# Four numbers of a hand-made instruction plan: the place of the last weight stores, and how far ahead loads are issued

## The chip, the core and the metric

The kernel runs on one core of a Trainium2 chip. The core has TensorE (PE, matrix products; PEld is its loading of the stationary operand), VectorE (DVE), ScalarE (ACT), GpSimd (POOL) and SyncE (SP). Here SP does nothing but issue transfers between memory and the core's buffers; 16 DMA engines carry them out. Each engine works through its own list of instructions in order and waits at an instruction until what it needs is there. The metric is device time of one launch in microseconds (us); the kernel before takes 1144.37 us, the median of 3 runs (1144.27 to 1144.45).

## What is computed

Two layers, each an attention block and a feed-forward block, run twice with the same weights, on 2048 rows of 640 numbers (float32). Cut to what matters:

```python
def _A_ref(x, wqkv, wo):              # 32 heads of 20, window of 8 rows, 2 apart
    qkv = x @ wqkv
    idx = pos[:, None] - off[None, :]                # off = 0, 2, ..., 14
    logits = einsum("bhsd,bhswd->bhsw", q, k[idx]) * scale   # masked where idx < 0
    attn = softmax(logits)
    return einsum("bhsw,bhswd->bhsd", attn, v[idx]) @ wo

def _B_ref(x, w1, b1, w2, b2):        # 640 -> 1536 -> 640
    y = layernorm(x)
    h = gelu(y @ w1 + b1)
    return h @ w2 + b2

x = x + _A_ref(layernorm(x), wqkv, wo)
x = x + _B_ref(layernorm(x), w1, b1, w2, b2)
x = x + _A_ref(layernorm(x), wqkv, wo)
x = x + _B_ref(layernorm(x), w1, b1, w2, b2)
```

## The kernel before, in words

**Numbers as pairs.** Every matrix operand is held as a pair of float16 numbers, a high part and the rest ("hi" and "lo"), and a product is three passes over such pairs. Weights come as float32, are split on the chip (ACT makes hi, DVE makes lo, both at line 475 and 476), and the pairs of the feed-forward weights are written to a scratch array `mw` in memory: 12 blocks of w1 (`mw[0][f]`) and 12 of w2 (`mw[1][f]`), each 320 KB. This is `prep_m`; its store is the transfer at line 517. Every feed-forward block later loads them back, block by block, at line 864.

**Units and stages.** The 2048 rows are 4 units of 512 rows (4 tiles of 128); over two layers that makes 8 unit-stages n = 0 to 7. Each has a layer norm, a product with wqkv (`qkv`, line 648 on PE), spilling of q, k and v to memory and fetching with shifted rows (lines 671 and 690), attention on DVE for 4 groups of heads (lines 732 to 770), the product with wo (line 805), a second layer norm, and a feed-forward part (`mlp`). Normalised rows are turned by a transposing transfer (line 620, `yT<-w`; line 793, `yT<-ohl`).

**One feed-forward part.** `mlp` runs over 12 blocks e of the 1536 inner columns. Block j = 12 * part + e needs a `c1` load (w1) for its inner product (line 871, `ps<-yT,c`, 15 matmuls), then GELU and hi on ACT (877, 880), lo on DVE (882), and a `c2` load (w2) for its outer product (line 892, `acc<-c,act`), which adds into five accumulator banks over all 12 blocks. Unit 0 of layer 1 is done as two parts of two tiles each (parts 0 and 1, inner matmuls of 256 columns), the next five units as one part each; the last two units are done together by another scheme (`pair`, lines 1073 and 1108). After the units from the fourth on, ACT copies the accumulator banks back to the rows (lines 916 and 926, priority `DRAIN`) and, for the next one, the rows into the banks (lines 853 and 855, priority `FILL`).

**Buffers.** There are 3 buffers `c1` and 3 buffers `c2`. Splitting uses them too: block f of w1 is split into a `c1` buffer and block f of w2 into a `c2` buffer, which come free when the stores to `mw` have landed. The users of `c1` and of `c2` get buffers in a fixed order: the 12 blocks of the splitting first, then the loads 0, 1, 2, ... of the feed-forward parts.

**The order of everything** is made before the launch by the class `Plan`. Each step is added with its engine, an estimated duration, a priority (lower goes first), what it needs, gives and uses. `Plan.run` then plays a simple model of the engines and the transfers, always takes the step that can start first (at the same time the one of lower priority), and emits the instructions of each engine in that order. The estimated times go no further than the order: on the chip each instruction waits only for the results and buffers that it needs, and for those ahead of it on its engine. Four things in this class matter here:

- A transfer marked `lazy` (rows of x, weights, bias, the stores to `mw`, the `c1` and `c2` loads) may not start in the plan before the transfers planned so far are within `AHEAD` us of being done. The others (spills, fetches of q, k and v, transposes, outputs) may.
- `SPARE[engine]` is added to the planned landing of a transfer for a step of that engine that needs it.
- `prio` of the splitting store is `prio - 5`, with `prio = 10 + f`: 5 for the first block, 16 for the last. `c1` and `c2` loads have -250 + j (+ 1.5 for c2), fetches -300 + group, spills -310 + n, the transposes of the feed-forward's layer norm -150 + n.
- The priorities of ACT's copies between rows and accumulator banks are `FILL` and `DRAIN`. Other steps of ACT near them: GELU -430, hi of GELU -440, the exponential of attention -450 + group, the copies before and after the product with wo (lines 817 and 822) -600 + n and -700 + n.

```python
            if o["lazy"]:
                t = max(t, seen - self.AHEAD + sum(x[0] * x[1] for q in queues.values() for x in q)
                        + sum(v["move"][0] * v["move"][1] for _, v in soon))
```

Of the kernel before, what the change touches and what calls it, by code (L numbers as in the profile page):

```python
# [18 lines left out]
NF = F // P  # L19
# [20 lines left out]

AHEAD = 1.5

# [23 lines left out]
PAIRS = ("qk", "pv", "ad", "o", "sub", "at", "hlo", "yl", "xb", "ol", "wq", "lo", "lm")  # L66

TURN = 2.7
FILL, DRAIN = -420, -700

THROUGH = (("sa", 29),)
LOP = ((29, -460),)
# [2 lines left out]
class Plan:  # L75
# [8 lines left out]
    SWITCH = 1.3  # L84


    AHEAD = 3.0
    REACH = 0.75
    LAND = 0.9
    RAMP = 0.2  # L90

    SPARE = {"pe": 2.0, "act": 1.5, "dve": 1.5, "pool": 0.7, "sp": 0.0}

    SHARE = 1.08

# [26 lines left out]
    def run(self):  # L122
# [64 lines left out]
        def start(o):  # L187
            t = clock[o["eng"]]
# [3 lines that stand above are left out]
            if o["pair"] and o["eng"] == "dve":  # L192
                t = max(t, port)
            for k in o["need"]:
                e, w, moved = when[k]
                w = w + (self.LAG["sp"] + self.SPARE[o["eng"]] if moved else self.LAG[e] if e != o["eng"] else 0.06 * (e != "pe"))
                t = max(t, w)
# [80 lines left out]
def packet_time(n):  # L278
    return 0.0075 + n / 26.9e3
# [11 lines left out]
def sliding_dilated_then_mlp_kernel(  # L291
# [18 lines left out]
    nc = tc.nc  # L310
# [41 lines left out]
    def tile_of(pool, key):  # L352
        return T[pool][plan.slot[pool, key]]
# [52 lines left out]
    mw = [[dram.tile([P, 2, D], HT, name=f"mw{i}{f}") for f in range(NF)] for i in range(2)]  # L406
# [16 lines left out]
    def dma(kb, prio, emit, need=(), give=(), use=(), by="sp", packet=4 * D):  # L423
        lazy = give[0][0] in ("x", "sq", "st", "c1", "c2", "zero", "mw", "raw", "rows", "d1", "mt") or give[0] in ("b1", "b2")
        plan.add(by, 0.1 if by == "act" else 0.38, prio, emit, need, give, use, move=(kb * 1e3 / 16 / packet, packet_time(packet)), lazy=lazy)
# [4 lines left out]
    def mm(cols, n, prio, emit, need=(), give=(), use=()):  # L430
        plan.add("pe", cols / 2400.0 + 0.0028 * n, prio, emit, need, give, use)
# [63 lines left out]
    def prep_rows(name, prio, src, hi, lo, use=()):  # L495
        key = (through[name], name)

        def load():
            st = tile_of(*key)
            w = src()  # L500
            nc.sync.dma_start(st.rearrange("p (k c) -> p k c", k=w.shape[1]) if len(w.shape) == 3 else st, w)

        dma(P * D * 4 / 1e3, prio, load, need=[("ev", 0, M - 1, 0)], give=[("st", name)], use=[key],
            packet=4 * P if name[0] == "m" and not name[2] else 4 * D)
        a, v = split(hi, lo, lambda: tile_of(*key))
        act(D, prio, a, need=[("st", name)], give=[("hi", name)], use=[key, *use])
        dve(D, next(p for n, p in LOP if blocks.index(name) < n), v, need=[("hi", name)], give=[("lo", name)], use=[key, *use])
# [4 lines left out]
    def prep_m(f, i, prio):  # L512
        ck = (f"c{i + 1}", ("prep", f))
        src = (lambda: B_w2[f * P:(f + 1) * P]) if i else (
            lambda: B_w1.rearrange("(k p) c -> p k c", p=P)[:, :, f * P:(f + 1) * P])
        prep_rows(("m", f, i), prio, src, lambda: tile_of(*ck)[:, 0], lambda: tile_of(*ck)[:, 1], [ck])
        dma(328, prio - 5, lambda: nc.sync.dma_start(mw[i][f], tile_of(*ck)),
            need=[("lo", ("m", f, i))], give=[("mw", f, i)], use=[ck])

    def turn(prio, t, name, key, nk, yk):  # L520
# [309 lines left out]
    def mlp(at, b, t0, t1):  # L830
# [28 lines left out]
        for e in range(NF):  # L859
# [7 lines left out]
            def inner(ck=ck, pk=pk):  # L867
# [6 lines left out]

            mm(3 * KD * nt, 15, j - 1.0 - AHEAD, inner, need=[*ready, ck, *split_done] + [("hhi", j - 2)] * (e > 1), give=[("hp", j)],
               use=[yk, ck, pk])
# [155 lines left out]
    def pair():  # L1032
# [68 lines left out]
        def first(bank, wt, todo, start, prio, need, give, use):  # L1101

            def product():
                ps = tile_of(*bank)
                k = 0
                for w0, z in todo:
                    for a, c in PASS:
                        nc.tensor.matmul(ps, wt()[:, a, w0:w0 + P], z(c), start=start and k == 0, stop=k == 3 * len(todo) - 1,  # L1108
                                         skip_group_check=True)
                        k += 1  # L1110

            mm(3 * len(todo) * BANK, 3 * len(todo), prio, product, need=need, give=give, use=[bank, *use])
# [3 lines left out]
        def yb(k):  # L1116
            return lambda c: transposed(yk)[:, c * KD + k]

        for e in R:
# [3 lines left out]
            if e == 0:  # L1123
                rows_in("P1", -284, lambda e: mw[1][e][:, :, :HALF], lambda e: [("mw", e, 1)])
            wt = partial(tile_of, *ck)
            after = [("wop", n1, M - 1, 1)] if e < 3 else []
            first(pk, wt, [(k * P, yb(k)) for k in range(KH)], True, j - 1.0 - AHEAD, [*ready, ck, *after] + [("hi", ("P1", e - 2))] * (e > 1),
                  [("P1", e)], [yk, ck])
            act(BANK, -441, lambda pk=pk, e=e: nc.scalar.activation(A21[e], tile_of(*pk), AF.Copy), need=[("P1", e), *free["pr"]],
                give=[("s1", e)], use=[pk])  # L1130
            first(pk, wt, [(k * P, yb(k)) for k in range(KH, KD)], False, j - 1.1 - AHEAD, [("s1", e)], [("C11", e)], [yk, ck])
            gelu(A11[e], partial(tile_of, *pk), e, ("h11", e), [("C11", e), *free["wo"]], [pk])
# [21 lines left out]
        for e in R:  # L1154
# [16 lines left out]
            B52, B51 = 10 * P, 11 * P  # L1171
            pr = j - 1.0 - AHEAD
            act(BANK, -436, lambda e=e, bk=bk: nc.scalar.activation(tile_of(*bk), A21[e], AF.Copy), need=[("s1", e), ("P1", NP - 1)],
# [174 lines left out]
```

## Time and profile before

| | |
|---|---|
| time, median of 3 runs | 1144.37 us |
| the profiled execution | 1147.83 us, of which the span from first to last instruction is 1146.1 us |
| PE busy | 1137.1 us, 99% of the span |
| DVE busy | 1038.4 us, 91% |
| ACT busy | 606.6 us, 53% |
| POOL busy | 113.2 us, 10% |
| DMA engines busy, queue of SP | 69.9% of 16 engines' span, 234.36 MB |
| mean granted clock of PE | 0.998 |

How to read the profile's lines in what follows. A row of the timeline gives the start in us, the time it covers, engine, line of the code, operation, output and inputs by the program's names (buffer numbers left out, so `c` is a buffer `c1` or `c2`), how many instructions are merged, and in brackets the idle time before it with what ended that. SPq rows are SP issuing transfers: their time is that of the issue, not of the transfer. A row of the windows gives, for a stretch of time, the busy time of each engine with its number of instructions, then the granted clock of PE as a share of full speed, the mean busy share of the DMA engines, and GB/s. A row of the waits gives who waited for whom, the total us, how often, and the longest.

### The profile page before, as it was taken

Reading aid. Unit: us, or ns where it says so; the run is one execution under the profiler, and the core shown is the slowest. Engines: PE = TensorE matmul, PEld = TensorE weight load, DVE = VectorE, ACT = ScalarE, POOL = GpSimd, SP = SyncE. Lnnn points to the kernel's source line nnn. Section 1 sums busy time; section 2 is a strip of 40 time slices with the busy share of each in tenths; the row PEclk is TensorE's granted clock in tenths of the full one; section 3 lists DMA queues with packets and bytes.
Section 4 is the critical chain, followed back from the end, with each engine's and each line's share of the span. In section 5 each row is a group of like instructions: output and inputs, shape, how many; then the busy total and the mean of one; then the engine's idle time right before and its main releaser. Section 6 shows DMA issues by size and latency. Waiting matters only on the chain.

```text
span 1146.1 us, 17470 instructions
## 1 busy us (share of the span) xinstructions
PE 1137.1 (99%) x6812; PEld 628.4 (55%) x6812; DVE 1038.4 (91%) x1028; ACT 606.6 (53%) x1131; POOL 113.2 (10%) x94
## 2 busy tenths in 40 slices
PE   9999999999999999999999999999999999999998
PEld 6444446567565465546555555556455556555476
DVE  7999999999899999999999999999999993847972
ACT  6485336536365275734537662479347445657720
POOL 1010000211111102110112012012111000000000
PEclk9999999999999999999999999999999999999999
DMA  9999998978976477576655965569686555974201
GB/s 318 307 299 266 329 302 244 321 264 244 239 189 232 140 221 213 178 207 198 186 187 176 221 190 164 175 188 192 164 247 183 175 171 156 217 239 122 65 24 69
DMA packets 239791, 235.47 MB, mean 205 GB/s; under 512 B 139020, under 2 KB 195164, under 8 KB 239708
## 3 DMA queue, kind: packets, MB, share of 16 engines
q1 hardware_dynamic: 239708, 234.36, 69.9%
q8 instruction: 53, 0.87, 0.3%
q14 instruction: 30, 0.25, 0.1%
HBM read 157.55 MB, written 44.78 MB: 177 GB/s over the span
## 4 chain that ended last, share of the span: by engine, by line
PE 72%; DVE 3%; DMA 1%; issue 0%; ACT 0%; DVEq 0%
PE acc L892 18%; PE ps L871 17%; PE ps L648 17%; PE ps L805 10%; PE acc L1073 4%; PE ps L1108 3%; PE ps L1073 2%; DMA yT<-w 1%; DVE yT L1020 1%; DVE pr L1005 1%; PE acc L1108 1%; DVE wq L1194 0%; DVE wq L1182 0%; DVE v L1195 0%; DVE xf L1196 0%
## 5 line engine op out<-in xcount | busy, mean ns | idle before, releaser
L648 PE MATMUL ps<-wq,yT 128*128 128x480 f16 (+1 forms) x1950 | 391.0, 363 | 1.5 <-DMA yT<-w 1.1
L648 PEld LDWEIGHTS <-yT 128*128 128x128 f16 x1950 | 189.3, 98 | 200.8 <-DMA yT<-w 1.4
L892 PE MATMUL acc<-c,act 128*128 128x512 f16 (+1 forms) x1728 | 249.3, 299 | 2.3 <-DMA c<-mw 1.6
L871 PE MATMUL ps<-yT,c 128*128 128x512 f16 (+1 forms) x1260 | 247.8, 350 | 0.0
L892 PEld LDWEIGHTS <-act 128*128 128x128 f16 x1728 | 136.1, 98 | 108.8 <-issue 1.9
L871 PEld LDWEIGHTS <-c 128*128 128x128 f16 x1260 | 120.9, 98 | 107.3 <-DMA c<-mw 0.3
L732 DVE TENSOR_TENSOR pr<-qk 128x2560 f32<-128x2560 f32 x64 | 179.5, 2808 | 0.0
L758 DVE TENSOR_TENSOR pr<-sm,v 128x2560 f32<-128x2560 f32 x64 | 179.1, 2818 | 0.3
L736 DVE TENSOR_REDUCE sm<-pr 128x128 f32<-128x2560 f32 x64 | 179.2, 2801 | 0.0
L665 ACT ACTIVATE ev<-ps 128x480 f32<-128x480 f32 x128 | 72.6, 568 | 177.2 <-PE ps L648 157.5
L877 ACT ACTIVATE act<-ps,b 128x512 f32<-128x512 f32 (+1 forms) x84 | 52.4, 624 | 172.9 <-PE ps L871 170.2
L766 DVE TENSOR_TENSOR pr<-pr 128x640 f32<-128x640 f32 (+1 forms) x128 | 143.1, 1150 | 0.3
L805 PE MATMUL ps<-wo,yT 128*128 128x320 f16 x960 | 131.7, 299 | 0.0
L805 PEld LDWEIGHTS <-yT 128*128 128x128 f16 x960 | 93.8, 98 | 37.4
L780 POOL TENSOR_TENSOR ohl<-w,ohl 128x640 f16<-128x640 f32 x24 | 34.9, 1456 | 425.9 <-DVE pr L732 171.6
L882 DVE TENSOR_TENSOR act<-act 128x512 f16<-128x512 f32 (+1 forms) x84 | 51.0, 609 | 16.0 <-ACT act L880 15.9
L587 POOL TENSOR_TENSOR ln<-ln,half 128x2 f32<-128x2 f32 (+1 forms) x31 | 36.2, 1173 | 276.6 <-ACT ln L584 276.6
L625 POOL TENSOR_TENSOR xf<-xf,b 128x640 f32<-128x640 f32 x24 | 37.3, 1558 | 144.6 <-DVE pr L732 58.4
L880 ACT ACTIVATE act<-act 128x512 f16<-128x512 f32 (+1 forms) x84 | 47.5, 565 | 3.4 <-PE acc L892 1.5
L610 ACT ACTIVATE w<-xf,ln 128x640 f32<-128x640 f32 x53 | 47.5, 909 | 2.7 <-DVE w L618 2.1
L570 ACT ACTIVATE junk<-xf 128x640 f16<-128x640 f32 x57 | 41.8, 733 | 12.9 <-DVE xf L814 8.0
L618 DVE TENSOR_TENSOR w<-w,w 128x640 f16<-128x640 f32 x56 | 45.7, 830 | 2.1 <-ACT w L616 2.1
(200 smaller groups left out, 984.1 us busy)
## 6 DMA issues: line engine op xcount, KB each, us to landing
c<-mw SPq DMA_DIRECT2D x174, 320.0 KB, 3.6
spill<-ev SPq DMA_DIRECT2D x64, 480.0 KB, 3.6
qk<-spill SPq DMA_DIRECT2D x32, 880.0 KB, 6.0
v<-spill SPq DMA_DIRECT2D x32, 880.0 KB, 5.3
qk<-spill SPq DMA_DIRECT2D x32, 320.0 KB, 3.6
act<-in_B_w_dram SPq DMA_DIRECT2D x24, 320.0 KB, 4.9
mw<-c SPq DMA_DIRECT2D x24, 320.0 KB, 4.7
pr<-in_B_w_dram SPq DMA_DIRECT2D x24, 320.0 KB, 4.1
```

The source lines that it names most:

```text
L648: nc.tensor.matmul(ps, transposed(yk)[:, a * KD + k, t * P:(t + 1) * P], wq[:, b, k, g, i0:i1], start=first and j == 0, stop=last and j == ...
L665: act(3 * GC, -400 + n, lambda i=i, pk=pk, ek=ek: nc.scalar.activation(tile_of(*ek)[:, :, i], tile_of(*pk)[:, :3 * GC].rearrange("p (a c) ...
L732: nc.vector.tensor_mul(tile_of(*pk), w[:, HALO + m + t0:HALO + m + t0 + EH, None, :].to_broadcast([P, EH, W, GC]), windows(w, t0, [GC, W], ...
L736: dve(E, G - 0.7, lambda pk=pk, t0=t0: nc.vector.tensor_reduce(lg(t0, t0 + EH).rearrange("p t w h -> p (t w h)"), tile_of(*pk).rearrange(" ...
L758: nc.vector.tensor_mul(tile_of(*vk).rearrange("p t w (h d) -> p t (w h) d", d=DH), lg(t0, t0 + EH).rearrange("p t w h -> p t (w h)")[:, :, ...
L766: dve(EH * w * GC, G - 0.9, lambda vk=vk, w=w: nc.vector.tensor_add(tile_of(*vk)[:, :, 0:w], tile_of(*vk)[:, :, 0:w], tile_of(*vk)[:, :, w ...
L805: nc.tensor.matmul(tile_of(*pk)[:, :D // 2], transposed(yk)[:, a * KD + k, t * P:(t + 1) * P], wo[:, b, k, c * D // 2:(c + 1) * D // 2], s ...
L871: nc.tensor.matmul(tile_of(*pk)[:, :nt], tile_of(*ck)[:, a, k * P:(k + 1) * P], transposed(yk)[:, c * KD + k, t0 * P:t1 * P], start=i == 0 ...
L877: act(nt, -430, lambda pk=pk, h32=h32, e=e: nc.scalar.activation(tile_of(*h32)[:, :nt], tile_of(*pk)[:, :nt], AF.Gelu_apprx_tanh, bias=b1[ ...
L882: dve(nt, -1000, lambda h32=h32, hk=hk: nc.vector.tensor_sub(tile_of(*hk)[:, 1, :nt], tile_of(*h32)[:, :nt], tile_of(*hk)[:, 0, :nt]), nee ...
L892: nc.tensor.matmul(accs[k][:, c0:c0 + n], tile_of(*hk)[:, a, (i - t0) * P:(i - t0 + 1) * P], tile_of(*wk)[:, c, w0:w0 + n], start=first, s ...
L1073: nc.tensor.matmul(tile_of(*to(i))[:, :HALF], hl()[:, a, i * P:(i + 1) * P], row(c), start=start and (a, c) == PASS[0], stop=(a, c) == PAS ...
```

## The change

Three numbers of the plan, and the priority of one pair of stores. `AHEAD` goes from 3.0 to 2.0 us, `SPARE` of ACT from 1.5 to 1.0 us, `DRAIN` from -700 to -450. The stores of the last block of the splitting (f = 11, of `mw[0][11]` and `mw[1][11]`) get priority -260 instead of 16; the other 22 keep theirs. No step of the plan is added or removed, and no data moves that did not move before; only orders change.

```diff
-FILL, DRAIN = -420, -700
+FILL, DRAIN = -420, -450
...
-    AHEAD = 3.0
+    AHEAD = 2.0
...
-    SPARE = {"pe": 2.0, "act": 1.5, "dve": 1.5, "pool": 0.7, "sp": 0.0}
+    SPARE = {"pe": 2.0, "act": 1.0, "dve": 1.5, "pool": 0.7, "sp": 0.0}
...
-        dma(328, prio - 5, lambda: nc.sync.dma_start(mw[i][f], tile_of(*ck)),
+        dma(328, -260 if f > NF - 2 else prio - 5, lambda: nc.sync.dma_start(mw[i][f], tile_of(*ck)),
             need=[("lo", ("m", f, i))], give=[("mw", f, i)], use=[ck])
```

## The prediction, made before the changed kernel was built

> **What bounds the kernel now.** I read the page first, then PE's waits, then windows and timelines of PE, DVE and SP around each wait.
>
> ```profile
> span 1146.1 us, 17470 instructions
> PE 1137.1 (99%) x6812; PEld 628.4 (55%) x6812; DVE 1038.4 (91%) x1028; ACT 606.6 (53%) x1131; POOL 113.2 (10%) x94
> ```
>
> PE is busy in all but 9.0 us, and the change leaves PE's work as it is. So a gain can only be idle time of PE, or time in which it runs slowly. These are its waits, all of them:
>
> ```profile
> PE acc L892 <- DMA c<-mw: 1.6, 2, 1.3
> PE acc L1269 <- POOL ident L447: 1.3, 1, 1.3
> PE ps L648 <- DMA yT<-w: 1.1, 1, 1.1
> PE acc L892 <- DVE act L882: 0.7, 1, 0.7
> PE acc L531 <- DVE w L606: 0.3, 1, 0.3
> PE ps L648 <- DVE yT L539: 0.2, 1, 0.2
> ```
>
> L1269, L531 and L539 belong to the first microseconds, before any feed-forward part. The others stand in two places, both in the first feed-forward unit. The first place, on PE:
>
> ```profile
> 234.37 1.80 PE L871 MATMUL ps<-yT,c 128*128 128x256 f16 x15
> ...
> 237.99 0.72 PE L892 MATMUL acc<-c,act 128*128 128x512 f16 x4 [0.73 <-DVE act L882]
> 239.97 1.05 PE L892 MATMUL acc<-c,act 128*128 128x512 f16 x4 [1.26 <-DMA c<-mw]
> 240.81 3.16 PE L871 MATMUL ps<-yT,c 128*128 128x256 f16 x15
> ...
> 244.90 1.80 PE L871 MATMUL ps<-yT,c 128*128 128x256 f16 x15
> ...
> 248.16 1.04 PE L871 MATMUL ps<-yT,c 128*128 128x256 f16 x8
> ```
>
> Undisturbed, one block (15 inner and 12 outer matmuls) takes 248.16 - 244.90 = 3.26 us. The inner products that start at 234.37 and 244.90 are two blocks apart, so 6.52 us of work took 10.53: **4.0 us are lost here**. Idle time is 0.73 + 1.26 = 2.0 of it. The rest is speed: the 15 inner matmuls at 240.81 take 3.16 us, the same 15 elsewhere 1.80. The windows show why, in the column behind POOL, the granted clock, followed by the DMA engines' share:
>
> ```profile
> 221.00:229.00 8.00, 8.00 (x69) 6.12 (x67) 8.00 (x9) 3.24 (x7) 0.20 (x1) 1.00 1.01 351
> 237.00:245.00 8.00, 6.00 (x34) 3.60 (x33) 8.00 (x9) 2.52 (x6) 1.40 (x1) 0.79 0.55 195
> 245.00:253.00 8.00, 8.00 (x71) 6.09 (x68) 8.00 (x8) 1.78 (x4) 1.66 (x1) 1.00 0.89 293
> ```
>
> The clock is 0.79 of full speed in the window of the stall and 1.00 on both sides. The DMA engines are full (1.01) up to 229, and half idle (0.55) in the stall itself, so what PE waited for was asked for late.
>
> The Trainium skill ("TensorE: Matmul & The Clock Gate", Part 1 on the HAM clock gate) has PE fall to half clock after an idle window of about 3.4 us. By that rule gaps of 0.7 and 1.3 us would not be enough; the trace has the fall behind them all the same, and the measurement decides.
>
> The second place:
>
> ```profile
> 281.77 7.96 SPq L620 DMA_TRANSPOSE yT<-w  x2
> 289.52 0.70 PE L892 MATMUL acc<-c,act 128*128 128x512 f16 x4 [0.35 <-DMA c<-mw]
> 291.30 8.88 PE L648 MATMUL ps<-wq,yT 128*128 128x480 f16 x43 [1.07 <-DMA yT<-w]
> ```
>
> Here 0.35 + 1.07 = 1.4 us are lost, to a load and to transposes, two of which hold SP's queue for 7.96 us.
>
> **Part 1: the stores of the last block go first.** SP before, each transfer named by lining SP's rows up with the order of the kernel's steps:
>
> ```profile
> 217.05 1.31 SPq L864 DMA_DIRECT2D c<-mw  x2
> 225.13 0.42 SPq L517 DMA_DIRECT2D mw<-c  x1
> 226.94 3.04 SPq L864 DMA_DIRECT2D c<-mw  x3
> 232.43 4.09 SPq L864 DMA_DIRECT2D c<-mw  x5
> 202.05 2.29 DVE L476 SCALAR_TENSOR_TENSOR c<-act,c 128x640 f16<-128x640 f32 x3
> c<-mw SPq DMA_DIRECT2D x174, 320.0 KB, 3.6
> mw<-c SPq DMA_DIRECT2D x24, 320.0 KB, 4.7
> ```
>
> The store at 225.13 is the last of the 24, that of w2's block 11. Its data is ready at 202.05 + 2.29 = 204.3, where DVE ends the last three splits; it then stands 20.8 us behind steps of lower number. Until it has landed (225.13 + 4.7 = 229.8) it holds one of the three `c2` buffers, and the first loads go round in the other two. So block 2's load waits for outer product 0 to free a buffer, block 3's for outer product 1 (it is the last of the three rows from 226.94, at about 229.7), and block 4's, the first of the five at 232.43, has the third buffer. PE waits for that one until 239.97.
>
> With priority -260 the store stands ahead of every `c1` and `c2` load (-250 and up) and of the layer norm's transposes (-150), behind spills and fetches. At the latest it goes in place of the loads at 217.05 and has landed by 217.05 + 4.7 = 221.8. Then block 2's load needs no outer product and goes near 221.8, block 3's moves to the moment when outer product 0 ends, and block 4's to that of outer product 1, 229.7: 2.7 us before 232.43. With the same journey it lands at 239.97 - 2.7 = 237.3. Undisturbed, PE wants it after inner product 5 (from 234.37) and outer product 3, one block later, at 234.37 + 3.26 = 237.6. It fits, barely; the burst of five that lengthens its journey is thinner too, as block 2's load left before. So the 1.26 goes, and the slow clock behind it.
>
> The 0.73 is DVE's order: the low part of block 3 comes behind a 2.82 us product of attention that the plan set first.
>
> ```profile
> 234.78 2.82 DVE L732 TENSOR_TENSOR pr<-qk 128x2560 f32<-128x2560 f32 x1
> 237.51 0.42 DVE L882 TENSOR_TENSOR act<-act 128x256 f16<-128x256 f32 x1
> ```
>
> That step has the strongest priority on DVE (-1000), so it can only be set behind where the plan expects its input late; with the `c2` loads earlier it expects it earlier. Bounds: 0 to 0.73 regained; I take all of it, since the same order arose from the same late buffer.
>
> What the store is moved past comes later by its issue, 0.42 us, and by 320 KB at 351 GB/s, 0.9 us of the DMA engines: block 2's `c1` load from 217.05 is wanted three blocks before the inner product at 234.37, at 234.37 - 3 * 3.26 = 224.6, so 7.5 us cover a journey of 3.6 and this 0.9. Without that cover it would cost the 0.9. The store of w1's block 11, the one before it, can move forward past a transpose or two; what covers that is the product with wqkv, which PE works on until the first inner products, in the window from 221. **Sum of part 1: -4.0 us**; from below -3.3, without the 0.73.
>
> **Part 2: AHEAD 3.0 to 2.0.** On the chip this changes only SP's order: spills, fetches and transposes that become ready within that microsecond go ahead of a load that could wait. The releasers of the loads, and the largest transfers:
>
> ```profile
> SPq L864 <- PE ps L871: 114.5, 52, 3.4
> SPq L864 <- PE acc L892: 113.2, 59, 4.3
> qk<-spill SPq DMA_DIRECT2D x32, 880.0 KB, 6.0
> ```
>
> 52 + 59 = 111 of the 174 `c` loads wait on SP until PE frees their buffer; the planned backlog hardly touches these. A buffer is wanted again 3 * 3.26 - 3.26 / 2 = 8.1 us after it came free, the load takes 3.6, so 4.5 us are to spare. One 880 KB fetch put ahead adds at most its own 6.0 - 3.6 = 2.4: hidden. Two add 4.8: not hidden. Bounds: -1.4 (the second place goes too, as its transposes meet a shorter queue) to +0.35 for each block whose load is overtaken twice. I take one such wait, **+0.35**, the nearest row (that at 289.52).
>
> **Part 3: SPARE of ACT, and DRAIN.**
>
> ```profile
> ACT ev L665 <- DMA act<-in_B_w_dram: 4.9, 2, 2.5
> L822 ACT ACTIVATE xf<-ps 128x320 f32<-128x320 f32 x56 | 24.0, 428 | 22.6 <-PE ps L805 22.2
> L926 ACT ACTIVATE xf<-acc 128x512 f32<-128x512 f32 x12 | 6.7, 598 | 0.2
> ```
>
> With less SPARE the plan sets a step of ACT that needs a transfer up to 0.5 us earlier, and ACT may stand there while evictions (line 665) queue behind it; PE would then lack a bank. ACT has already stood 4.9 us in this way without a wait of PE's, so another 0.5 is hidden by the banks that are full; bounds 0 to 0.5. The 12 copies of line 926 may now fall behind the copies of the wo product: 8 in a unit, 8 * 0.43 = 3.4 us, and behind them wait the refill of the banks and the next unit's first outer product. The cover is PE's inner products and the next qkv. Bounds: 0 to 3.4; I take 0 for both, as no wait of PE's now comes from ACT.
>
> **The sum.** Of the profiled execution: 1147.83 - 4.0 + 0.35 = 1144.2 (span 1142.5, and 1.7 around it). The runs' median is 3.46 below that execution, so the forecast is 1144.37 - 3.65 = **1140.7 us**. The gain survives only if PE remains what ends last:
>
> ```profile
> 950.00:975.00 25.00, 25.00 (x171) 16.08 (x170) 8.52 (x18) 15.59 (x37) 0.69 (x1) 1.00 0.52 134
> 1050.00:1075.00 25.00, 24.94 (x126) 12.07 (x124) 24.25 (x41) 17.54 (x28) 0.00 (x0) 1.00 0.37 113
> ```
>
> Near 950 DVE is through with attention and then idle for 25 - 8.52 = 16.5 us, with PE full: DVE has room to be overtaken.
>
> **Rivals.** *Idle time alone returns.* If unprofiled runs do not fall to the slow clock, they regain 2.0 and not 4.0: 1144.37 - 2.0 + 0.35 = 1142.7. For it: no row tells the clock of an unprofiled run. Against: in the trace the fall follows the gaps at once. The skill's rule on the clock speaks for this rival, as it asks for a longer gap.
>
> *DVE sets the pace.* DVE is busy 8.00 of 8.00 from 221 to 253. PE, 4 us ahead, meets results of attention that are not, and waits the gain away: 1144.4. For it: between 1050 and 1075 DVE is busy 24.25 of 25 and PE already lacks 0.06. Against: the 16.5 us, and a list of waits with only 0.7 + 0.3 + 0.2 for DVE.
>
> *Loads starve* (slower). In the first unit's two parts PE takes two loads of 320 KB every 3.26 us, 196 GB/s, beside spills and fetches, with the DMA engines at 0.89 to 1.01 where PE is not stalled. If the new order sets two fetches or transposes ahead of the loads there as a rule, each of the 24 blocks waits like that at 289.52: 24 * 0.35 = 8.4, and 1144.37 - 4.0 + 8.4 = 1148.8. It decides from 4.5 us of added journey. For it: the row at 281.77, where two transposes alone held the queue for 7.96. Against: the 111 loads that wait for buffers and not for the queue.
>
> **How the numbers follow.** The forecast has 0.62 and its own range from 1139.0 (the second place's 1.4 regained, no new wait) to 1142.1; idle time alone 0.10; DVE 0.09; starving loads, or one uncovered copy of part 3, 0.19. A measurement of this kernel tells about 0.2% from no change, 2.3 us; faster means under 1142.1: 0.62 and 0.04 of the second case, 0.66; same 0.06 + 0.09 = 0.15; slower 0.19. The range takes in 0.5 us below the forecast's own and the slower cases up to a quarter of the starving one, 1144.37 + 2.1: 1138.5 to 1146.5.
>
> **What would show it.** Right: the last of the 24 stores issued before 218, and the `c2` load of block 2 before 223; from 221 on inner products at steps of 3.26 us with a clock of 1.00; no `acc <- DMA c<-mw` wait over 0.5 us; a span near 1142.5. Wrong: many such waits between 221 and 372 (starving), waits of PE for DVE from 300 on (pace), or for ACT's lines 853, 916 and 926 (DRAIN).

## The result, and the profile after

| | before | after |
|---|---|---|
| time, median (range, runs) | 1144.34 us (1144.25 to 1145.03, 6) | 1149.55 us (1147.47 to 1150.39, 6) |
| ratio, 95% interval | | 1.0039, 1.0029 to 1.0049 |
| profiled execution | 1147.83 us, span 1146.1 | 1148.08 us, span 1146.3 |
| the same, profiled once more | 1144.33 us, span 1142.6 | 1149.34 us, span 1147.6 |

The change makes the kernel slower by 0.4%, about 5 us. The forecast was 1140.7 us, faster, and the range ended at 1146.5. The last row holds the first surprise: profiled again, the unchanged kernel takes what its median says, 3.5 us less than in the profile that the prediction was made from.

The page of the changed kernel, span and busy times:

```profile
span 1146.3 us, 17474 instructions
PE 1135.8 (99%) x6812; PEld 628.2 (55%) x6812; DVE 1040.3 (91%) x1028; ACT 604.5 (53%) x1131; POOL 127.2 (11%) x94
```

The engines do the same work, with one exception: GpSimd (POOL) is busy for 127.2 us in place of 113.2, with the same 94 instructions. Most of that are four additions (L625, `xf<-xf,b`), which take 4.05 to 6.87 us here and at most 1.66 before; no wait on them is in the profile. PE's waits in the changed kernel (who waited for whom, us in all, times, longest):

```profile
PE ps L648 <- DMA yT<-w: 1.5, 2, 1.1
PE ps L805 <- ACT ps L817: 1.4, 2, 0.7
PE acc L1269 <- POOL ident L447: 1.3, 1, 1.3
PE ps L871 <- DMA c<-mw: 1.3, 1, 1.3
PE ps L648 <- ACT yT L537: 1.2, 1, 1.2
PE ps L805 <- DMA yT<-ohl: 0.2, 1, 0.2
```

Beside them the same view of the unchanged kernel, profiled the second time:

```profile
PE acc L1269 <- POOL ident L447: 1.4, 1, 1.4
PE acc L892 <- DVE act L882: 0.7, 1, 0.7
PE acc L892 <- DVE xf L936: 0.6, 1, 0.6
PE acc L531 <- DVE w L606: 0.5, 1, 0.5
PE ps L648 <- DVE yT L539: 0.2, 1, 0.2
PE ps L648 <- DMA yT<-w: 0.2, 1, 0.2
```

No wait for a `c` load is left in that list: the 1.26 us that the change was to remove, and the slow clock behind them, belonged to the execution profiled first. New in the changed kernel are waits on the copies into the banks of the wo product (L817), for which the kernel before never waits, and longer ones on transposes. They stand at 635 to 639, 787 and 854 us, the second half, from which the prediction's sum took no term.

What the store did. SP's rows in the changed kernel around the last stores:

```profile
210.93 0.57 SPq L517 DMA_DIRECT2D mw<-c  x1
212.04 0.53 SPq L517 DMA_DIRECT2D mw<-c  x1
...
225.64 0.52 SPq L517 DMA_DIRECT2D mw<-c  x1
```

The rows at 210.93 and 212.04 are the two stores of block 11, early as predicted. But one of the 22 stores that kept their priority now stands where the last one stood: at 225.64 it is w2's block 10, whose data was ready at 204.0 (rows lined up with the order of the kernel's steps). It holds a `c2` buffer until 225.64 + 4.3 = 229.9, where before block 11's held it until 229.8. Block 2's `c2` load goes at 228.5, before it went at 228.0. And PE still waits in that place:

```profile
236.51 2.34 PE L892 MATMUL acc<-c,act 128*128 128x512 f16 x16
240.13 1.81 PE L871 MATMUL ps<-yT,c 128*128 128x256 f16 x15 [1.28 <-DMA c<-mw]
```

The 0.73 for DVE is gone, 1.28 for a load has come. The clock stays at 1.00 around it, in the window from 237 to 245:

```profile
237.00:245.00 8.00, 6.72 (x56) 4.75 (x55) 8.00 (x10) 2.71 (x6) 1.40 (x1) 1.00 0.72 241
```

**Where the time went.** The stretch that tells it lies 390 us later. Timeline rows of the changed kernel, first GpSimd and DVE, then ACT, then PE:

```profile
621.39 6.92 POOL L587 TENSOR_TENSOR ln<-ln,half 128x2 f32<-128x2 f32 x1 [9.02 <-ACT ln L584]
617.32 5.56 DVE L758 TENSOR_TENSOR pr<-sm,v 128x2560 f32<-128x2560 f32 x2
622.79 0.69 DVE L882 TENSOR_TENSOR act<-act 128x512 f16<-128x512 f32 x1
623.39 4.36 DVE L766 TENSOR_TENSOR pr<-pr 128x1280 f32<-128x1280 f32 x4
631.20 0.83 DVE L618 TENSOR_TENSOR w<-w,w 128x640 f16<-128x640 f32 x1 [3.45 <-ACT w L616]
...
628.35 0.48 ACT L592 ACTIVATE ln<-ln 128x1 f32<-128x1 f32 x2 [4.40 <-POOL ln L587]
...
635.47 3.21 PE L648 MATMUL ps<-wq,yT 128*128 128x480 f16 x15 [0.36 <-DMA yT<-w]
639.78 3.21 PE L648 MATMUL ps<-wq,yT 128*128 128x480 f16 x15 [1.10 <-DMA yT<-w]
```

GpSimd's power (L587, the inverse deviation of a layer norm) works on 128 x 2 numbers. It starts at 621.39, while DVE runs its large products, and ends at 628.31, half a microsecond after DVE's last add (623.39 + 4.36 = 627.75). It was kept out until DVE stopped. And DVE stops because its next step needs what that power releases: 3.45 us of idle time on an engine that has none to give. The same place in the unchanged kernel, with another order of the same steps:

```profile
617.84 0.95 POOL L587 TENSOR_TENSOR ln<-ln,half 128x2 f32<-128x2 f32 x1 [8.40 <-ACT ln L584]
...
614.82 2.81 DVE L758 TENSOR_TENSOR pr<-sm,v 128x2560 f32<-128x2560 f32 x1
617.56 0.68 DVE L882 TENSOR_TENSOR act<-act 128x512 f16<-128x512 f32 x1
618.16 1.48 DVE L766 TENSOR_TENSOR pr<-pr 128x1280 f32<-128x1280 f32 x1
```

There the power comes 0.2 us behind the end of a product and takes 0.95 us. The Trainium skill ("SBUF — State Buffer", section "SBUF: two separate sides") says that DVE, with two inputs in SBUF, and GpSimd share a pair of ports as an exclusive lock, held for a whole instruction. By that rule the power would wait for the end of the product that was running, at 622.88; the trace shows it waiting through that boundary and five more instructions.

How much DVE has to give is one row of windows, from 200 to 860 us (busy time of PE, PEld, DVE, ACT, POOL in that order, with the number of instructions). The unchanged kernel:

```profile
200.00:860.00 660.00, 658.47 (x4012) 365.92 (x4011) 650.29 (x556) 352.09 (x670) 89.82 (x64) 1.00 0.70 207
```

The changed kernel:

```profile
200.00:860.00 660.00, 655.62 (x3987) 363.02 (x3986) 645.58 (x550) 341.83 (x652) 99.52 (x59) 1.00 0.70 205
```

PE is full to 99.8% before, DVE to 98.5%: two engines fill this stretch, and neither has much room for a delay. After, DVE has done 650.29 - 645.58 = 4.7 us less in the same time, and the span is 3.7 us longer. Where PE loses its part is plain from 600 to 900 us, first the unchanged kernel, then the changed one:

```profile
600.00:900.00 300.00, 300.00 (x1768) 160.78 (x1767) 294.65 (x246) 174.14 (x332) 38.48 (x28) 1.00 0.67 192
```

```profile
600.00:900.00 300.00, 297.13 (x1742) 158.62 (x1741) 292.67 (x239) 167.05 (x326) 46.60 (x28) 1.00 0.66 189
```

PE stands still for 300 - 297.13 = 2.87 us there, before for none. Over the whole span it stands still for 10.5 us, before for 7.3, so nearly all of the difference of 3.2 lies in this stretch. (In the other profile of the changed kernel it is 2.83 us here and 1.0 more than before between 200 and 300.)

### The profile page after: what moved, and what is told of

It reads as the page before. It is cut to its first block, busy times and chain, and to the rows that moved or that the text cites. A ratio compares the mean times of both kernels' runs of the same rounds, so it can differ in the third digit from the quotient of the medians.

```text
span 1146.3 us, 17474 instructions
## 1 busy us (share of the span) xinstructions
PE 1135.8 (99%) x6812; PEld 628.2 (55%) x6812; DVE 1040.3 (91%) x1028; ACT 604.5 (53%) x1131; POOL 127.2 (11%) x94
## 4 chain that ended last, share of the span: by engine, by line
PE 74%; DVE 15%; issue 4%; DMA 3%; ACT 2%; POOL 2%; SPq 0%; DVEq 0%; POOLq 0%; ACTq 0%
PE ps L648 26%; PE acc L892 15%; PE ps L871 15%; PE ps L805 10%; PE acc L1073 3%; PE ps L1108 3%; DVE pr L732 3%; DVE pr L758 2%; DVE pr L766 2%; PE ps L1073 2%; DVE sm L736 1%; DVE act L882 1%; DVE pr L1005 1%; DMA yT<-ohl 1%; POOL ln L587 1%
## 5 line engine op out<-in xcount | busy, mean ns | idle before, releaser
L780 POOL TENSOR_TENSOR ohl<-w,ohl 128x640 f16<-128x640 f32 x24 | 37.3, 1556 | 360.4 <-DVE pr L732 130.0
L625 POOL TENSOR_TENSOR xf<-xf,b 128x640 f32<-128x640 f32 x24 | 50.2, 2095 | 189.6 <-DVE pr L732 101.5
L587 POOL TENSOR_TENSOR ln<-ln,half 128x2 f32<-128x2 f32 (+1 forms) x31 | 34.0, 1100 | 279.5 <-ACT ln L584 279.4
L882 DVE TENSOR_TENSOR act<-act 128x512 f16<-128x512 f32 (+1 forms) x84 | 52.7, 630 | 6.7 <-ACT act L880 6.7
```

The costliest lines, as they stand in the source:

```text
L882: dve(nt, -1000, lambda h32=h32, hk=hk: nc.vector.tensor_sub(tile_of(*hk)[:, 1, :nt], tile_of(*h32)[:, :nt], tile_of(*hk)[:, 0, :nt]), nee ...
```

## The experiments

Ratios are to runs of the kernel before taken with them (medians 1144.77 to 1145.14), with 95% intervals. Where a kernel has lines added, its line numbers are higher by the lines added ahead of them.

**1. The parts alone and together.** First the kernel before, unchanged, to see what a second profile shows.

> The kernel before once more, unchanged, for a second profile on the chip of the other runs. If the 4.0 us stall at 237 to 244 belongs to every execution, the span is again near 1146 and the stall is there. If it belongs to the first profile only, as the gap of 3.46 us between that execution and the median suggests, the span is near 1142.5, PE's waits for the c loads between 230 and 245 stay under 1 us in all, and the clock does not fall.

Measured 1144.54 us (11 runs), ratio 1.0001 [0.9992, 1.0009], profiled execution 1144.33. Its waits are shown above. The granted clock is 1.00 in ten of the 11 runs, and 0.999 in that of 1148.62 us; it was 0.998 in the execution profiled first.

Only the stores:

```diff
-        dma(328, prio - 5, ...
+        dma(328, -260 if f > NF - 2 else prio - 5, ...
```

> Only the stores of block 11 get priority -260. Stores theory (the prediction's part 1): the stall between 230 and 245 goes, 1140.7 if every execution has it, about 1143 if not. The plan's own model expects 1.1 us more than before (it ends at 1147.1 instead of 1146.0): 1145.4. AHEAD theory (the loss sits in AHEAD alone): within 1 us of before.

Measured 1148.1 us, 1.0033 [1.0021, 1.0045]. Here the store of w2's block 11 is the last of the 24, at 217.4, and block 2's `c2` load goes at 224.8: what part 1 of the prediction describes. But block 1's `c2` load, which stood at 217.36, now goes at 222.75, and PE waits for it at 228:

```profile
PE acc L892 <- DMA c<-mw: 2.4, 1, 2.4
```

Only `AHEAD`:

```diff
-    AHEAD = 3.0
+    AHEAD = 2.0
```

> Only AHEAD 3.0 to 2.0. AHEAD theory: the whole loss is here, 1149 to 1150. SPARE theory (the loss comes from ACT steps set too near to the transfers they need): within 1 us of before, 1144. The plan's own model expects 1.2 us less, 1143.1.

Measured 1148.55 us, 1.0035 [1.0023, 1.0047]; waits of 0.7 to 1.3 us on loads, transposes and DVE, spread over 226 to 293.

Only ACT's `SPARE`:

```diff
-    SPARE = {"pe": 2.0, "act": 1.5, ...
+    SPARE = {"pe": 2.0, "act": 1.0, ...
```

> Only SPARE of ACT 1.5 to 1.0. SPARE theory: the whole loss is here, 1149 to 1150, with PE waiting for ACT at line 817 as in the changed kernel (1.4 us there). AHEAD theory: within 1 us of before, 1144. The plan's own model expects 0.5 us less, 1143.8.

Measured 1148.11 us, 1.004 [1.0023, 1.0057]. `DRAIN` alone changes the order of no engine, nor does it beside any of the other parts, so it had no run.

The stores with `AHEAD`:

> Stores first and AHEAD 2.0, SPARE as before. If effects of the parts add up, this is the run with the stores plus the run with AHEAD, less before. AHEAD theory: 1149 to 1150. SPARE theory: 1144. The plan's own model: 1.2 us less than before, 1143.1.

Measured 1148.43 us, 1.0031 [1.0019, 1.0043].

The stores with `SPARE`:

> Stores first and SPARE 1.0, AHEAD as before. AHEAD theory: within 1 us of before, 1144. SPARE theory: 1149 to 1150. The plan's own model: no difference, 1144.3.

Measured 1146.19 us, 1.0018 [1.0009, 1.0026].

`AHEAD` with `SPARE`:

> The change without its stores: AHEAD 2.0 and SPARE 1.0. If the stores do what the prediction says, this is slower than the changed kernel, by 1 to 4 us: 1151 to 1154. The plan's own model: 2.6 us more than before and 4.9 more than the changed kernel. If no part has an effect of its own and each order meets its own stalls, it lies anywhere between 1143 and 1152, and the sum of the parts' effects misses it by over 2 us.

Measured 1150.45 us, 1.0049 [1.0037, 1.0061].

The whole change again:

> The changed kernel on this chip, beside the three above. As on record: 1147.5 to 1150.4, about 5 us over before. PE's waits: some 1.4 us for a c load near 238, 1.8 for transposes near 635, 0.9 and 0.8 for line 817 of ACT near 786 and 853; the times vary by up to 3 us from one execution to the next.

Measured 1149.34 us (1146.07 to 1151.79, 11 runs), 1.0036 [1.0026, 1.0045]. The power takes 6.91 us here too, and DVE stands still for 3.45 us behind it.

What follows: the three parts alone cost 0.33, 0.35 and 0.40%, which would add up to 1.08%; together they cost 0.36 to 0.39%, and two of them together 0.18 to 0.49%. So no part has a price of its own. Each draws a new order of the plan's 3704 steps, and the price is that of the order. Nor do the parts lose it where the whole change does: from 600 to 900 us PE stands still for 0.0 (stores), 0.0 (`AHEAD`) and 0.5 us (ACT's `SPARE`), against 2.9 with the whole change; from 200 to 600 us for 4.4, 5.0 and 3.1, against 1.5 in the unchanged kernel and 1.5 and 2.6 in the two profiles of the changed one.

**2. The store by hand.** To have the moved store without a new order, single steps were set at another place of the finished order of the kernel before, by this code with a list of moves (reference step, behind or ahead of it, steps):

```python
    order = plan.run()
    step = {k: o for o in order for k in o["give"]}
    for j, (ref, d, keys) in enumerate(MOVES):
        for i, k in enumerate(keys):
            step[k]["at"] = step[ref]["at"] + d * 1e-4 * (len(keys) - i if d < 0 else i + 1)
    order.sort(key=lambda o: o["at"])
```

```diff
+    (("c1", 2), -1, [("mw", 11, 1)]),
```

> The order of the kernel before, with one row moved by hand: the store of w2's block 11 stands ahead of the two loads at 217 on SP, and nothing else changes place, on SP or on any other engine. Order theory (a change of the numbers costs through all the orders that it redraws, not through the step that it names): within 0.5 us of before, 1144.5. Store theory (the store itself holds up the loads behind it): PE waits 2 to 2.5 us for a c load near 228 as with the stores' priority alone, 1147 to 1148.

Measured 1145.0 us, 0.9996 [0.9987, 1.0005]. The store itself is worth nothing, in either direction. Block 2's `c2` load keeps its place on SP behind three others and still goes at 228.1, so this run prices the moved store alone, not the earlier load that part 1 added to it. The profiled execution, at 1146.05 the slowest of the 11, holds a wait of 1.9 us for another `c` load at 263.

The same, with block 1's `c2` load as late as the stores alone had put it:

```diff
+    (("put", 3, 3, 1), 1, [("c2", 1)]),
```

> The order of the kernel before with two rows moved by hand on SP: the store of w2's block 11 ahead of the loads at 217, and the c2 load of block 1 behind the spill at 222, which is where the plan with the stores' priority alone put it. If that load, displaced by the plan's limit on what may wait, is the stall at 228, PE waits 2 to 2.5 us there and the time rises by 2 to 3.5 us, 1146.5 to 1148. If the stall came from other orders of that plan, within 0.5 us of the kernel with the store alone.

Measured 1144.93 us, 0.9999 [0.999, 1.0008]. PE waits for that load, 0.6 us and not the 2 to 2.5 that were expected, and the kernel's time does not show it.

**3. PE's waits mended one by one.** The kernel before, with three of its waits taken away by moving the step that is late:

```diff
+    (("hlo", 3), 1, [("qk", 7, 0)]),
+    (("xr", 1, 0, 0), 1, [("lg", 8, 0)]),
+    (("qkvp", 4, 0, 0), -1, [("outh", 0, 6, 3), ("out", 0, 6, 2), ("out", 0, 6, 3)]),
```

> The kernel before with its own three remaining stalls mended by hand: on DVE the product qk of group 7 behind the low part of block 3, and the sum of group 8 behind the drain of the shared bank; on PE three outer products of block 18 ahead of the product with wqkv of unit 4. If the stalls are orders, 0.9 + 0.8 + 0.3 us go: 1142.5, and DVE's waits on PE's list are gone. If each mended stall comes back at the next place, 1144.5.

Measured 1147.62 us, 1.0023 [1.0012, 1.0035]: slower. The mended waits are gone, and a new one of 1.7 us stands at 286. SP in that kernel:

```profile
277.01 0.32 SPq L870 DMA_DIRECT2D c<-mw  x1
282.36 0.32 SPq L696 DMA_DIRECT2D v<-spill  x1
282.80 0.35 SPq L870 DMA_DIRECT2D c<-mw  x1
```

The fetch at 282.36 waits for a buffer that DVE's attention frees, and the load that PE needs stands behind it on SP. So what was taken from DVE's attention most likely came back through SP's queue; no run shows it apart.

The changed kernel with four of its waits mended the same way, all in the order of DVE, PE and ACT:

```diff
+    (("xr", 1, 0, 0), 1, [("lg", 8, 0)]),
+    (("qkvp", 4, 0, 0), -1, [("outh", 0, 6, 3), ("out", 0, 6, 2), ("out", 0, 6, 3)]),
+    (("qkvp", 6, 0, 0), -1, [("outh", 3, 3, 3)] + [("out", 3, 3, i) for i in range(4)]),
+    (("yh", ("a", 7), 3), -1, [("xw", 5, 2, 0)]),
```

> The changed kernel with four of its stalls mended by hand in the same way: on DVE the sum of group 8 behind the drain of the shared bank (1.6 us at 268), on PE three outer products ahead of the wqkv product of unit 4 (1.1 of 1.3 us at 297) and five ahead of that of unit 6 (1.6 us at 636), on ACT the fill of a bank ahead of a conversion that waits for GpSimd (1.0 us at 787). Order theory: 5.3 us less than the changed kernel, 1144.0, about the kernel before. If the loss sits in the loads themselves (AHEAD theory: every load a little late), the same 1149, with new waits for c.

Measured 1153.17 us, 1.0065 [1.0052, 1.0079], the slowest of all. PE's idle time from 626 to 645 falls from 1.46 us to 0.07, the wait at 787 grows to 3.0:

```profile
PE ps L812 <- ACT ps L824: 4.7, 3, 3.0
```

and DVE's busy time from 200 to 860, third of the busy times, is the lowest of the kernels made from the changed one:

```profile
200.00:860.00 660.00, 653.50 (x3971) 361.57 (x3969) 644.07 (x549) 339.86 (x648) 107.03 (x59) 1.00 0.70 205
```

**4. Is it the direction, or any new order?** Three kernels that move one constant of the plan in another way than the change does.

```diff
-    AHEAD = 3.0
+    AHEAD = 3.2
```

> The kernel before with AHEAD 3.2 in place of 3.0, the opposite direction of the change: loads may be issued farther ahead of an empty queue. The plan's own end moves from 1145.6 to 1144.9. Theory 'a redrawn order costs, whichever way it was redrawn' (the order of before is one that ran well, and the plan's small gains are not seen by the chip): slower, 1146.5 to 1150, with PE waits of 0.5 to 3 us at the ends of transfers and at handovers from ACT and DVE that are in no profile of before. Rival 'the direction is what costs' (loads closer to an empty queue starve PE): 1143.5 to 1144.6, no new waits.

Measured 1149.84 us, 1.0047 [1.0029, 1.0064]. Here loads that may go earlier cost as much as loads that must wait.

```diff
-    SPARE = {"pe": 2.0, "act": 1.5, "dve": 1.5, ...
+    SPARE = {"pe": 2.0, "act": 1.5, "dve": 1.4, ...
```

> The kernel before with the spare time that the plan leaves before a DVE step fed by a transfer at 1.4 in place of 1.5 us: none of the constants of the change is touched. The plan's own end moves from 1145.6 to 1144.2. Theory 'a redrawn order costs': slower, 1146.5 to 1150. Rival 'the change's own constants cost': 1143.5 to 1145.

Measured 1146.77 us, 1.0013 [1.0004, 1.0023]: slower, at the lower end of what the theory gave.

```diff
-ASIDE = 1.7
+ASIDE = 1.75
```

> The kernel before with the length that the plan gives to one kind of GpSimd step at 1.75 in place of 1.70 us: the order is the same up to 506 us and redrawn behind it; the plan's own end moves from 1145.6 to 1146.0. Theory 'a redrawn order costs': slower by 0.5 to 3 us, less than the others since only the second half is redrawn, the waits of PE new behind 506 us and unchanged ahead of it. Rival 'what costs lies at the spill and the second pass of the weights, at 200 to 300 us': no change, 1144 to 1145.

Measured 1144.64 us, 0.9997 [0.9989, 1.0006]. The theory that any new order costs falls here, and the rival's 1144 to 1145 holds: an order that is new behind 506 us only, and that leaves DVE's busy time from 200 to 860 at 650.16, costs nothing. The plan's own end is no guide: it comes 0.7 us earlier with `AHEAD` 3.2, 1.4 with DVE's `SPARE` and 2.3 with the whole change, all of them slower, and 1.1 later with the stores alone, also slower.

**5. GpSimd's blocked rows.** In the changed kernel six GpSimd rows take 3.7 us or more; before, the longest takes 3.45. Four are the additions of L625, at 246, 335, 449 and 808 us. The other two stand just ahead of waits of PE's: the power at 622 and a subtraction (L780) at 783, 3.77 us. These two were mended by moving steps of DVE:

```diff
+    (("yl", ("a", 6), 0), 1, [("ad", 19, 0, 4), ("ad", 19, 1, 4), ("ad", 19, 0, 2), ("ad", 19, 1, 2)]),
+    (("yl", ("a", 7), 2), 1, [("pv", 25, 0)]),
```

> The changed kernel with two places of its order mended by hand on DVE. Place one: four adds of group 19 (L766) go behind the first low-half subtraction of unit 6 (L618), so that DVE leaves a gap while GpSimd's power of that unit (L587, 128x2, 6.9 us at 622.7 in the changed kernel) waits for it. Place two: the product of group 25 (L758) goes behind the third low-half subtraction of unit 7, so that GpSimd's subtraction for group 24 (L780, 3.77 us at 783.4) runs before it. Theory 'blocked GpSimd': both GpSimd rows fall to under 1.5 and about 1.4 us, PE's waits at 636 (yT, 1.65 us) and at 787 (ACT L817, 1.2 us) are gone or under 0.3 each, and the span falls by 2 to 3 us against the changed kernel's, to a median of 1146 to 1147.5. Rival 'the waits move on': the GpSimd rows get short, but PE waits elsewhere instead and the median stays at 1148.5 to 1150. Rival 'not the port': the power stays above 4 us though DVE stands idle.

Measured 1150.03 us, 1.004 [1.0028, 1.0052]. Both rows are short (the power 2.03 us, where under 1.5 was expected), and the waits at 636 and 787 are gone. The time is what it was. GpSimd, DVE and PE in that kernel:

```profile
623.52 2.03 POOL L592 TENSOR_TENSOR ln<-ln,half 128x2 f32<-128x2 f32 x1 [9.02 <-ACT ln L589]
783.41 1.40 POOL L785 TENSOR_TENSOR ohl<-w,ohl 128x640 f16<-128x640 f32 x1 [11.46 <-DVE w L623]
628.81 0.82 DVE L623 TENSOR_TENSOR w<-w,w 128x640 f16<-128x640 f32 x1 [3.22 <-ACT w L621]
855.48 2.74 PE L810 MATMUL ps<-wo,yT 128*128 128x320 f16 x19 [2.48 <-ACT ps L822]
```

The first theory (the blocked rows are the loss) falls; the waits moved on, to 855. DVE's row fits that: it stood still nearly as long as before, 3.22 us for 3.45, only earlier. What PE pays at 855 is a chain from DVE. In the changed kernel it reads:

```profile
850.74 0.42 DVE L745 TENSOR_TENSOR sm<-sm 128x256 f32<-128x256 f32 x1
851.20 0.42 ACT L747 ACTIVATE sm<-sm 128x256 f32<-128x256 f32 x1 [6.42 <-DVE sm L745]
851.63 1.28 ACT L877 ACT_TABLE_LOAD   x1
852.93 0.69 ACT L877 ACTIVATE act<-ps,b 128x512 f32<-128x512 f32 x1
853.51 1.15 ACT L817 ACTIVATE ps<-xf 128x320 f32<-128x320 f32 x3
854.00 4.24 PE L805 MATMUL ps<-wo,yT 128*128 128x320 f16 x30 [0.67 <-ACT ps L817]
```

ACT waits 6.42 us for DVE's softmax of group 28, loads its table, and only then comes to the copies that PE's wo product needs. In the unchanged kernel DVE is through with the same step at 844.4.

**6. DVE's idle time shortened, not moved.** So the next two runs start again from the changed kernel, leave DVE's steps where they are and let DVE stop for the power alone: its first add waits for it, and the four adds then run while ACT makes the rows. (The move in the first line only lists the power ahead of the add that refers to it; the order of instructions on all five engines is that of the changed kernel.)

```diff
+    (("hlo", 51), 1, [("rr", ("a", 6), 0)]),
...
+BEHIND = {("ad", 19, 0, 4): ("rr", ("a", 6), 0)}
...
+        for k in o["give"]:
+            if k in BEHIND:
+                tc.add_manual_dep(o["ins"], step[BEHIND[k]]["ins"].name,
+                                  mybir.DependencyInfo(mybir.DependencyClass.Sync, mybir.DependencyReason.DATA), reason="port")
```

> The changed kernel with one dependency more: DVE's first add of group 19 (L766) waits for GpSimd's power of unit 6 (L587), so that DVE stands still for about 0.7 us and then goes on with its four adds while ScalarE makes the rows that the power releases. Nothing is moved. Theory 'DVE's lost time is PE's': DVE's idle time at 629 falls from 3.45 us to under 0.5, with 0.5 to 1 us at 625 in its place; the maximum of group 28 (L744, at 851.4 in the changed kernel, 851.6 with the order mended) comes 2 to 3 us earlier; PE's waits at 636 and at 852 to 854 fall under 0.4 each, that at 787 stays near 1.2, and the median falls by 1.5 to 2.7 us, to 1146.6 to 1147.9. Rival 'the waits move on whatever DVE does': the power is short, DVE's idle time is less, but PE waits as long elsewhere and the median stays at 1148.7 to 1150.

Measured 1147.25 us (1145.68 to 1149.54, 11 runs), 1.0022 [1.0013, 1.0031]. GpSimd and DVE at the power, then GpSimd and PE 150 us later:

```profile
621.69 2.63 POOL L592 TENSOR_TENSOR ln<-ln,half 128x2 f32<-128x2 f32 x1 [9.02 <-ACT ln L589]
624.36 4.37 DVE L771 TENSOR_TENSOR pr<-pr 128x1280 f32<-128x1280 f32 x4 [0.59 <-POOL ln L592]
628.64 0.82 DVE L623 TENSOR_TENSOR w<-w,w 128x640 f16<-128x640 f32 x1
...
779.71 3.77 POOL L785 TENSOR_TENSOR ohl<-w,ohl 128x640 f16<-128x640 f32 x1 [9.90 <-DVE w L623]
777.70 14.46 PE L810 MATMUL ps<-wo,yT 128*128 128x320 f16 x104
```

0.59 us of idle time in place of 3.45. The wait at 787 is gone too, against the expectation: GpSimd's subtraction is as blocked as before, 3.77 us, and PE runs past it with 104 matmuls in a row. So that row alone does not make PE wait there: the wait is gone with the row mended (above) and with DVE's lag shortened (here). Group 28's maximum, 850.1 and 851.4 in the two profiles of the changed kernel and 851.6 with the blocked rows mended, comes at 847.7. One wait added saved 2.1 us against the changed kernel's 1149.34, as the theory said; of PE's waits at 852 to 854 it left 0.7, where under 0.4 was expected. The intervals of the two ratios still touch, between 1.0026 and 1.0031. Taken together, each run over the median of the kernel before in its own session, the 17 runs of the change average 1.0039 and the 20 with the gap (this kernel and the next) 1.0023: 1.8 us apart, with a standard error of about 0.5. The profiled execution is the fastest of its 11, so its span flatters the gap by about 1.6 us; what it shows is the place: PE's idle time from 600 to 900 is 0.69 us, against 2.87 and 2.83.

With the second of the two moves above as well:

```diff
+    (("yl", ("a", 7), 2), 1, [("pv", 25, 0)]),
```

> The same, and the product of group 25 (L758) goes behind the third low-half subtraction of unit 7 (L618), which in the run with both places mended took PE's wait at 787 away and cost DVE 0.87 us of idle time. Theory 'DVE's lost time is PE's': no PE wait above 0.4 us at 787, up to 0.5 us at 852, the median at 1146 to 1147.5, so little or nothing better than with the one dependency. Rival 'the waits move on': 2 to 3 us of wait at 852 and a median of 1148.7 to 1150.

Measured 1147.12 us, 1.0022 [1.0012, 1.0032]. There was no wait of PE's left to mend, and DVE stands still for 1.08 us there: nothing is gained, and the size of the first run is borne out. PE waits 1.0 us at 852, where up to 0.5 was expected; from 600 to 900 that is all it loses.

DVE's row of the windows in the run with the blocked rows mended, and in that with the gap:

```profile
200.00:860.00 660.00, 654.45 (x3978) 362.27 (x3977) 645.02 (x550) 339.98 (x649) 92.29 (x59) 1.00 0.70 205
```

```profile
200.00:860.00 660.00, 657.88 (x4004) 364.82 (x4003) 648.12 (x552) 344.35 (x657) 95.61 (x59) 1.00 0.71 206
```

Set beside the spans, all against the unchanged kernel's second profile (650.29 us of DVE, span 1142.6):

| kernel | DVE's work missing, 200 to 860 | span longer by |
|---|---|---|
| the change, both profiles | 4.7, 4.6 | 3.7, 5.0 |
| four of PE's waits mended | 6.2 | 6.0 |
| GpSimd's blocked rows mended | 5.3 | 5.2 |
| gap for the power | 2.2 | 1.3 |
| gap and second move | 3.5 | 2.7 |
| before, the profile of the prediction | 3.4 | 3.5 |
| store by hand; with the late load | 1.7; 0.1 | 1.7; 0.4 |
| `AHEAD` 3.2; `ASIDE` 1.75 | 5.0; 0.1 | 4.1; 0.2 |
| stores; stores and `SPARE` | 2.7; 5.6 | 4.6; 6.3 |
| `AHEAD`; `AHEAD` and stores; `AHEAD` and `SPARE` | 7.7; 7.4; 2.9 | 4.4; 4.8; 6.5 |
| ACT's `SPARE`; DVE's `SPARE` 1.4 | 5.0; 0.3 | 3.3; 2.4 |
| three waits of before mended | -0.7 | 1.7 |

In the orders made from the changed one and from the one before by hand, the span follows DVE's missing work within about 1 us, but for the last row. Among the orders that a constant has redrawn it does so in some and is off by 1.7 to 3.6 us, to either side, in six: there DVE also stands idle where nothing waits for it, or PE loses its time directly, to loads, transposes and handovers between 225 and 415. The table alone does not show which engine makes the other wait; the gap, which adds a wait of DVE's and shortens its idle time, does, for the stretch behind 620 in the changed kernel.

## Why the prediction was wrong, point by point

**"The sum" counted one stall twice.** It took 4.0 us off the profiled execution, which was 3.46 us above the median, and then took nearly the same 3.65 off the median. The second profile of the unchanged kernel settles it: 1144.33 us, PE at full clock, and 0.7 us of wait at 237 in place of 4.0 lost. Its 11 runs went from 1144.33 to 1148.62, with a clock of 1.00 in ten; the execution profiled first, at 1147.83 and 0.998, would be the second slowest of them. The median never held the stall. The sign was there to be read: a stall of 4.0 us in an execution that is 3.46 above its median is most likely what sets the two apart. What was to be had in this place was the 0.7 us, less than a measurement tells from no change.

**Part 1, the last store.** "the last of the 24 stores issued before 218" and "the `c2` load of block 2 before 223" both failed (225.64 and 228.5). The step looked only at the steps that the store is moved past; it did not ask which store comes last once block 11's is first. With the stores alone both held nearly (217.4 and 224.8), and there the step "what the store is moved past comes later by its issue, 0.42 us, and ... 0.9 us" failed: it costed a `c1` load at 1.3 us, while block 1's `c2` load was put off by 5.4 (217.36 to 222.75) and PE waited 2.4; the part put at -4.0 us cost 3.8 (0.0033 * 1144.5). The late load is not all of that wait, as by hand it gives 0.6. By hand, in an order that is otherwise the old one, the moved store gives 0.9996: its worth was nought. "The 0.73", DVE's order, was right: it is gone.

**Parts 2 and 3** were costed as single waits at a fixed order: +0.35, and 0 because "no wait of PE's now comes from ACT". Alone they cost 4.0 (0.0035 * 1144.5) and 4.6 us (0.004 * 1144.5), not by one wait of the kind that was costed, but by several of 0.2 to 1.3 us on loads, transposes, ACT and DVE: each of the two constants redraws the order of every engine. That term, a new order of two full engines, was missing from the sum. L817 is a wait of PE's on ACT, 1.4 us in the changed kernel, and the half of it at 854 comes from DVE, as the chain above shows. `DRAIN` was rightly costed at 0.

**The rivals.** *DVE sets the pace*, with 0.09, had the mechanism for the stretch behind 620: PE "meets results of attention that are not" ready, and its sign, waits of PE for DVE from 300 on, stands in the profile from 635 on, by way of ACT and of transposes. Its price was wrong. It ended at 1144.4, no gain, as if DVE itself went on at its old pace; DVE lost 4.7 us of work from 200 to 860, and the gap shows that PE pays for what it loses at 628. For the parts alone this rival does not hold: they lose before 600. The 16.5 us of room near 950 were real and irrelevant: that is behind the stretch in which DVE is the bound. *Loads starve* had the sign and, at 1148.8, the size, by a mechanism that is not there: one wait for a `c` load over 1 us in the changed kernel, against 24 that it counted. *Idle time alone returns* falls with the stall.

**What stays open.** Why the power was not let in at 622.79 in the changed kernel, where a product ends and the step of L882 begins, when it got through beside the same sequence (product, L882, add) in the kernel before. And the last 2.4 us: in the profile with the gap PE still loses 0.8 us at 239, 0.2 at 287, 0.4 at 297 and 0.7 at 851, of which the first three are no more than the unchanged kernel loses between 200 and 300; and DVE waits 1.49 us at 294 for a fetch whose product the new order sets 11 us earlier; none of these was tried alone, and why a slower execution of the same kernel is slower is not shown. Nor is it shown why each part alone costs about 4 us before 600. No kernel here beats the one before.

## What to carry to other kernels

Before a stall is taken off the time, ask whether the time holds it: when a profiled execution lies above the median by about the size of its largest stall, profile again. Where two engines are both over 98% busy in a stretch, price a change by what it does to the busy time of each of them there, and mend waits by shortening the idle time of the one that is behind; moving a wait out of sight moves it to the next handover. A change to a constant of a scheduler can change the whole order, and its cost is found by neighbours (the constant moved the other way, another constant, a late redraw), not by following one step.

## What the runs showed of the hardware that was not expected

- A GpSimd power on 128 x 2 numbers took 0.69 us in the best case, 0.95 beside DVE's product, L882 and add in the kernel before, and 6.92 beside the same kinds of steps in the changed order, where it got through when DVE stopped. Letting DVE stop for 0.59 us brought it to 2.63.
- The granted clock was 0.79 over 8 us in two profiles: in the first, behind waits of 0.73 and 1.26 us within 3 us, and with the stores alone, from 229 to 237, behind one of 2.40 us, where 15 inner matmuls took 2.39 us in place of 1.80 (a third longer). Behind a wait of 1.28 us in the changed kernel it stayed at 1.00. The rule of the Trainium skill cited in the prediction ("TensorE: Matmul & The Clock Gate", Part 1), a fall after an idle window of about 3.4 us, agrees with the last and not with the first two.
